# Attention and a routed expert layer on one core: fewer steps on which routing is advanced, a first token list over two groups, and first weights and transposes at other places of a DMA queue

## The chip, the core and the metric

The program runs on one core of a Trainium2 chip. Its engines work side by side, each on an instruction stream of its own, and wait for one another through semaphores: TensorE (PE in the profile, its weight loads PEld), VectorE (DVE), ScalarE (ACT), GpSimd (POOL) and SyncE (SP), which here issues nearly all DMA transfers. The metric is the device time of one execution in microseconds; lower is better.

## The reference

```python
def _attn_ref(q, k, v):                       # 8 x 8 heads, 1152 positions, 64 wide
    q_pool = q.reshape(B, H, S // 2, 2, D).mean(axis=3)       # 576 queries
    scores = scale * np.matmul(q_pool, k.transpose(0, 1, 3, 2))
    scores = scores - np.max(scores, axis=-1, keepdims=True)
    attn = np.exp(scores)
    attn = attn / (np.sum(attn, axis=-1, keepdims=True) + 1e-09)
    return np.matmul(attn, v)

def _moe_ref(x, modality_id, w_gate, modality_bias, w1, w2):  # x: 4608 tokens x 512
    logits = x @ w_gate + modality_bias[modality_id]
    e_idx = np.argmax(logits, axis=1)                         # one of 8 experts
    gate_w = softmax(logits)[arange(N), e_idx]
    for e in range(E):
        mask = e_idx == e
        h = np.maximum(x[mask] @ w1[e], 0.0)                  # w1: 512 x 1024
        out[mask] = gate_w[mask, None] * (h @ w2[e])          # w2: 1024 x 512
```

All is float32. The 64 heads' results, put side by side, are the 4608 tokens of 512 values that the second half routes, each to the one expert with the largest logit.

## The kernel before

**Attention.** Two heads share the 128 partitions, so there are 32 pairs (`npairs`), and each pair takes 18 steps (`NSTEP`) of a schedule written out by hand: 576 steps in all. PE computes the scores of a pair (`psc`, L906 and L907), takes the maximum of a coarser score pass for the pair after it (`pm`, L839 and L847, whose maxima DVE reduces at L840 and L848), and multiplies the exponentials with the values (`xp`, L965 to L967). Values in float32 are carried as pairs of 16-bit parts, a high and a low one. ACT makes the exponentials (`Pe`, L908) and part of their low parts (`Pl`, L889, and in pairs 26 and 27, `P_LIST`, some that DVE makes elsewhere); DVE makes the others (L891), the values' low parts (`vl`, L782, and `VS`, L798) and the output (L983 to L988). POOL adds the query halves (`split_q`, L658), splits them (`qh`, L667, `lo`, L695) and scales the values (`VH`, L786). SP copies all of these into the operands `B` and `QB` (`place`, L628), loads the next pairs (`load_kq`, `load_v`) and writes the row of maxima `mr` into `B` (`put`, L820). Since L907 reads that row, the pair's scores wait for it.

`hold` (L618) ties a POOL operation to a DVE one so that it comes after it; it is used for `split_q` and the first two `lo` of the pairs above `HELD` = 3.

**Scales.** Once per pair `scales` (L752) makes powers of two from a maximum, by four DVE operations `power_of` (L757): `sc` and its inverse `isc` for the values and the output, `isc` once more for the routing's table `scales`, and half of a tile `both` for the logits' weights.

**Logits.** After an odd pair, two heads' outputs are split (`split_x`, L935), turned by two DMA transposes (`turn_part`, L949) and multiplied with the routing weights (18 matmuls, L271) in the next pair. The first transpose is issued at once, at the end of the step of the ACT split; the second is left in `turns` and issued behind the next row DMA of `put`.

**Routing.** The tokens form four groups of 1152 (8 heads each, so a group is full after each 8 pairs). `Router` holds the code that turns logits into lists of tokens by expert: `setup` (L178, constants by 27 POOL operations, at once, at step 24), `route` of each group, and `first_list` (L569) after group 2: owners and sizes of the first six blocks of 256 tokens (`first_blocks`), the place of each token of three groups (`place`), and `listing`, per group three one-hot tables `ol` (L515), a table `o` (L521), two `r` (L526, L527) and nine matmuls (L547). These are generators in a list `side`. At the end of each of the 576 steps the first of them is advanced by a piece if its wait is over; what it yields is the wait in steps. A negative number is a step counted from the end: `T_LIST` = -127 puts the listing at step 449.

**The last pair and the experts.** At the step before the last pair, `gather_first` (L1579) runs what is left in `side` and issues the gather of the first block's tokens out of `xs`, a table in DRAM. At steps 1, 2, 3 and 3 of the last pair (`T_W0`) the four loads of the first expert's weights (512 KB each) are issued; ACT and DVE split them into parts at steps 6, 4, 10 and 11 (`split_first`, L1599 and L1601). Then 18 blocks of 256 tokens and half a block run through the two layers, PE by PE: `ph` (L1316 to L1318) and `po` (L1423 to L1425).

The order within each engine is the program's own: the schedule's steps decide it, and an engine takes no later instruction while an earlier one waits.

Of the kernel before, what the change touches and what calls it, by code (L numbers as in the profile page):

```python
# [9 lines left out]
F32 = mybir.dt.float32  # L10
# [12 lines left out]
P = 128  # L23
# [5 lines left out]
S = 1152  # L29
# [12 lines left out]
HELD = 3  # L42
BANK = W3 // 4
T_LIST = -127
# [77 lines left out]
T_W0 = (1, 3, 2, 3)  # L122
# [43 lines left out]
class Router:  # L166
# [11 lines left out]
    def setup(self, ids, w_gate, bias):  # L178
# [4 lines left out]
        for i in range(3):  # L183
            nc.gpsimd.tensor_copy(self.wg[:, :, i], wg)
            if i < 2:
# [5 lines left out]
        self.mid = con.tile([P, NTT], F32, name="mid")  # L191
        nc.gpsimd.tensor_copy(self.mid, idt[:, :, 0])
        self.up = con.tile([P, P], BF16, name="up")
        nc.gpsimd.memset(self.up, 1.0)
        nc.gpsimd.affine_select(out=self.up, in_=self.up, pattern=[[1, P]], compare_op=ALU.is_gt, fill=0.0, base=0, channel_multiplier=-1)
        self.id16 = con.tile([P, P], F16, name="id16")
        nc.gpsimd.tensor_copy(self.id16, self.ident)
        self.on = con.tile([P, P], BF16, name="on")
        nc.gpsimd.memset(self.on, 1.0)
        self.ie = self.iota("ie", E)  # L200
        self.ieE = self.iota("ieE", E, base=-E)
        self.lane16 = con.tile([P, P], BF16, name="lane16")
        nc.gpsimd.tensor_copy(self.lane16, self.iota("lane", P))
        self.part = self.iota("part", 1, cm=1)
        self.tile1 = self.iota("tile1", NTT, base=1)
        self.col = self.iota("col", 2 * (NBF - NA) + E)
        self.before = con.tile([P, E + 1, E], F32, name="before")
        nc.gpsimd.memset(self.before, 1.0)
        nc.gpsimd.affine_select(out=self.before, in_=self.before, pattern=[[1, E + 1], [-1, E]], compare_op=ALU.is_gt, fill=0.0, base=0,
                                channel_multiplier=0)  # L210
# [5 lines left out]
        self.added = {g: 0 for g in range(NTT // NT)}  # L216
        z = con.tile([P, NT, 2], F32, name="z")
        nc.gpsimd.memset(z, 0.0)
        nc.sync.dma_start(out=self.xs[T - NT * P:T, DM:XW].rearrange("(t p) d -> p t d", p=P), in_=z)
        self.pos = con.tile([P, NTT], F32, name="pos")  # L220
        self.exp = con.tile([P, NTT], F32, name="exp")
# [18 lines left out]
    def token_scale(self, p, isc):  # L240

        g, h = divmod(p, H)
        if h == 0:
            self.scales[g] = self.keep.tile([P, H], I32, name="scales")
        isc(self.scales[g][:, h:h + 1])
# [130 lines left out]
    def first_blocks(self):  # L376
# [29 lines left out]
        ef = sm.tile([P, NA], F32, name="ownA")  # L406
# [162 lines left out]
    def first_list(self):  # L569

        for _ in self.first_blocks():
            yield 1
# [1085 lines left out]
```

## Time and profile before

| | us |
|---|---|
| median of 3 runs (lowest, highest) | 1127.4 (1127.33, 1129.1) |
| the profiled execution | 1126.72 |
| its span, from first to last instruction | 1125.0 |
| PE busy, its mean granted clock | 1102.0, 0.997 |
| DVE, ACT, POOL busy | 972.0, 913.3, 414.2 |
| attention: a bare pair with logits, without | 22.16, 21.61 |
| the pair from 598.07 to 622.35, from 667.41 to 691.89 | 24.28, 24.48 |
| start of the last pair, of the experts' first matmul | 713.5, 735.3 |

How to read it: times are microseconds from the span's first instruction. A row of windows gives the stretch, its length, and for PE, PEld, DVE, ACT and POOL the busy time with the instruction count, then PE's granted clock, the share of the DMA engines and GB/s. A timeline row gives start, duration, engine, line, operation, what is written from what, and in brackets the idle time before it with what ended it. Pairs are cut here at the starts of ACT's squares (L743), one in each pair.

### The profile page before, as it was taken

What the parts mean: (1) busy time and instruction counts of PE and PEld (TensorE: products, weight loads), DVE (VectorE), ACT (ScalarE), POOL (GpSimd) and SP (SyncE); (2) the same over time, 40 slices, a digit from 0 to 9 for tenths busy, and PEclk for the clock granted to TensorE, in tenths of its full rate; (3) what the DMA queues carried; (4) which work ended last, traced back from release to release, by engine and by line L of the source; (5) the groups of instructions that cost most, each with busy time, mean ns of one, the idle gap of its engine ahead of it and who ended that gap; (6) DMA issues with size and microseconds to landing.
All of it is one profiled execution on the core that took longest, in us unless ns stands there. A gap on an engine that the chain in (4) does not pass through costs nothing.

```text
span 1125.0 us, 36836 instructions
## 1 busy us (share of the span) xinstructions
PE 1102.0 (98%) x15069; PEld 812.7 (72%) x15069; DVE 972.0 (86%) x1971; ACT 913.3 (81%) x1465; POOL 414.2 (37%) x408
## 2 busy tenths in 40 slices
PE   7999999999999999999999999999999999999997
PEld 3777777777777777777777777777667667667665
DVE  7999999999999999999999999877996766756755
ACT  5999999999999999999999998876556656655654
POOL 7753344355434444443445334115213112122111
PEclk9999999999999999999999999999999999999999
DMA  7777757768669578678687663499999999899993
GB/s 231 181 186 169 197 159 189 188 158 187 171 165 210 152 176 183 165 185 182 171 183 171 160 147 97 144 302 289 285 264 278 299 286 267 279 280 262 296 269 110
DMA packets 175522, 232.67 MB, mean 207 GB/s; under 512 B 92303, under 2 KB 126751, under 8 KB 175344
## 3 DMA queue, kind: packets, MB, share of 16 engines
q1 hardware_dynamic: 169254, 210.45, 71.4%
q0 software_dynamic: 6080, 19.78, 6.7%
q8 instruction: 120, 1.97, 0.8%
q14 instruction: 58, 0.48, 0.1%
q10 hardware_dynamic: 10, 0.00, 0.0%
HBM read 146.11 MB, written 18.99 MB: 147 GB/s over the span
## 4 chain that ended last, share of the span: by engine, by line
PE 80%; DVE 16%; DMA 2%; issue 1%; ACT 1%; SPq 0%; POOL 0%; POOLq 0%; DVEq 0%
PE psc L907 9%; PE psc L906 9%; PE pm L839 8%; DVE mp L840 8%; PE xp L965 6%; PE xp L967 6%; PE ph L1318 6%; PE ph L1316 6%; PE ph L1317 6%; PE xp L966 6%; PE po L1423 6%; PE po L1425 6%; PE po L1424 6%; DVE Pl L891 2%; DVE vl L782 1%; DVE mp L848 1%
## 5 line engine op out<-in xcount | busy, mean ns | idle before, releaser
L908 ACT ACTIVATE Pe<-psc 128x432 int32<-128x432 f32 x768 | 376.8, 526 | 40.6 <-PE psc L907 32.2
L840 DVE TENSOR_REDUCE mp<-pm 128x1 f32<-128x512 f32 x566 | 371.6, 684 | 16.8 <-PE pm L839 10.1
L965 PE MATMUL xp<-VH,Pe 128*128 128x65 f16 x2880 | 372.5, 193 | 0.0
L967 PE MATMUL xp<-VS,Pl 128*128 128x65 f16 x2880 | 371.9, 193 | 0.4 <-DVE Pl L891 0.4
L966 PE MATMUL xp<-vl,Pe 128*128 128x64 f16 x2880 | 370.6, 192 | 0.0
L966 PEld LDWEIGHTS <-Pe 128*128 128x128 f16 x2880 | 267.6, 98 | 87.6
L906 PE MATMUL psc<-B 128*128 128x432 f16 (+2 forms) x1152 | 304.1, 286 | 1.7 <-ACT Pe L908 1.5
L907 PE MATMUL psc<-B 65*128 65x432 f16 (+2 forms) x1152 | 304.7, 287 | 0.7 <-DMA B<-mr 0.5
L965 PEld LDWEIGHTS <-Pe 128*128 128x128 f16 x2880 | 272.0, 98 | 42.3 <-issue 4.7
L967 PEld LDWEIGHTS <-Pl 128*128 128x128 f16 x2880 | 266.5, 97 | 0.6 <-DVE Pl L891 0.6
L889 ACT ACTIVATE Pl<-Pe 128x1152 f16<-128x1152 uint16 (+1 forms) x190 | 219.2, 1154 | 6.0
L839 PE MATMUL pm<-hi,QB 128*128 128x512 f16 x566 | 213.8, 379 | 4.2 <-DVE mp L840 3.0
L1318 PE MATMUL ph<-xpart,w1l 128*128 128x256 f16 x544 | 148.3, 273 | 0.0
L1317 PE MATMUL ph<-xpart,w1h 128*128 128x256 f16 x544 | 148.3, 273 | 0.0
L1316 PE MATMUL ph<-xpart,w1h 128*128 128x256 f16 x544 | 148.3, 273 | 0.0
L786 POOL TENSOR_SCALAR VH<-rawv,sc 128x512 f16<-128x512 f32 (+1 forms) x60 | 103.6, 1736 | 76.2 <-PE pm L839 35.6
L907 PEld LDWEIGHTS <-B 65*128 65x128 f16 x1152 | 112.9, 98 | 25.2 <-issue 2.5
L906 PEld LDWEIGHTS <-B 128*128 128x128 f16 x1152 | 112.5, 98 | 7.9 <-issue 2.5
L1322 DVE SCALAR_TENSOR_TENSOR hl<-ph,hh 128x512 f16<-128x512 f32 x72 | 49.6, 689 | 76.6 <-ACT hh L1321 71.7
L1321 ACT ACTIVATE hh<-ph 128x512 f16<-128x512 f32 x72 | 43.0, 598 | 85.1 <-PE ph L1318 85.0
L1425 PE MATMUL po<-w2h,hl 128*128 128x512 f16 x288 | 109.2, 379 | 0.0
L1424 PE MATMUL po<-w2l,hh 128*128 128x512 f16 x288 | 109.2, 379 | 0.0
(288 smaller groups left out, 1881.3 us busy)
## 6 DMA issues: line engine op xcount, KB each, us to landing
w2r<-in_w_dram SPq DMA_DIRECT2D x76, 512.0 KB
w1r<-in_w_dram SPq DMA_DIRECT2D x72, 512.0 KB
rawv<-in_att_dram SPq DMA_DIRECT2D x32, 576.0 KB
B<-hi SPq DMA_DIRECT2D x128, 144.0 KB
rawq<-in_att_dram SPq DMA_DIRECT2D x31, 576.0 KB
rawk<-in_att_dram SPq DMA_DIRECT2D x31, 576.0 KB
B<-qh SPq DMA_DIRECT2D x128, 72.0 KB
B<-lo SPq DMA_DIRECT2D x64, 144.0 KB
```

The lines of the kernel that those rows point to most:

```text
L839: nc.tensor.matmul(pm, QB[p % 2][:, u], s["hi"][:, t * 512:(t + 1) * 512], start=True, stop=True)
L840: nc.vector.tensor_reduce(mp[:, u, t:t + 1], pm, op=ALU.max, axis=AX.X)
L889: nc.scalar.activation(low, rest, AF.Copy, scale=LOW)
L906: nc.tensor.matmul(o, b1[:, ks], b1[:, qs], start=True, stop=False, skip_group_check=True)
L907: nc.tensor.matmul(o, b2[:, ks], b2[:, qs], start=False, stop=True, skip_group_check=True)
L908: nc.scalar.activation(Pe[:, D + x0:D + x1], pt, AF.Exp, scale=1.0 / 16)
L965: nc.tensor.matmul(out, Ph[:, qs], vh[:, c, j, 0:D + 1], start=c == 0 and g == 0, stop=False, skip_group_check=True)
L966: nc.tensor.matmul(out[:, 0:D], Ph[:, qs], vl[:, c, j], start=False, stop=False, skip_group_check=True)
L967: nc.tensor.matmul(out, Pl[:, qs], vs[:, c, j, 0:D + 1], start=False, stop=c == NKC - 1, skip_group_check=True)
L1316: nc.tensor.matmul(o, hi[:, c, fs], xh[:, :, c], start=c == 0, stop=False)
L1317: nc.tensor.matmul(o, hi[:, c, fs], xl[:, :, c], start=False, stop=False)
L1318: nc.tensor.matmul(o, lo[:, c, fs], xh[:, :, c], start=False, stop=c == 3)
```

## The change

- `HELD` is 2 in place of 3: pair 3's q-addition and `lo` are held as well.
- `setup` becomes a generator in pieces with four steps between them (`ST`); its first piece runs at step 24 and the rest goes through `side`.
- The first list covers two groups (`GA`). `first_place` (sizes, owners and places) follows the routing of group 1, and `first_list`, now only the owners' last operation and the listing, that of group 2. `T_LIST` is gone.
- A piece of `side` comes only at eight steps of a pair (`QUIET`).
- `scales` makes two powers, the second straight into the routing's table, and POOL copies it to `both`.
- Both transposes wait in `turns` for the row DMA.
- The four weight loads are issued together, at the step 12 before the last pair, and behind the last pair's last key copy; their tiles are taken one step earlier.

```diff
-HELD = 3
+HELD = 2
+ST = 4
-T_LIST = -127
+GA = 2
+QUIET = (1, 2, 3, 4, 13, 14, 15, 16)
-T_W0 = (1, 3, 2, 3)
+T_W0 = -12
+T_R0 = -13
...
+        yield
+        self.up = con.tile([P, P], BF16, name="up")
+        nc.gpsimd.memset(self.up, 1.0)
+        nc.gpsimd.affine_select(out=self.up, in_=self.up, pattern=[[1, P]], ...)
+        yield ST
...
+    def first_place(self):
+
+        for _ in self.first_blocks():
+            yield PL
+        for _ in self.place(GA * NT, False):
+            yield PL
+
     def first_list(self):
 
-        for _ in self.first_blocks():
-            yield 1
-        for _ in self.place(3 * NT, False):
-            yield PL
-        yield T_LIST
+        self.ownA = self.con.tile([P, NA], I32, name="ownerA")
+        self.nc.vector.tensor_single_scalar(self.ownA, self.efA, float(E - 1), op=ALU.min)
+        yield 1
         acc = self.con.tile([P, 2, 2 * NA], F32, name="accA")
-        yield from self.listing(3, 2 * NA, acc)
+        yield from self.listing(GA, 2 * NA, acc)
...
-                move(s["B1"][half[i], kcol(j)], s["hi"][half[j]])
+                s["placed"] = move(s["B1"][half[i], kcol(j)], s["hi"][half[j]])
...
-        sc = sm.tile([P, 2], I32, name="sc")
+        sc, isc = sm.tile([P, 1], I32, name="sc"), on_scale(p)
-        power_of(sc[:, 0:1], half, -1, 205)
-        power_of(sc[:, 1:2], half, 1, 49)
-        on_scale(p, lambda o: power_of(o, half, 1, 49))
+        power_of(sc, half, -1, 205)
+        power_of(isc, half, 1, 49)
-        power_of(st[p - p % 2]["both"][r], half[r], 1, 49)
+        nc.gpsimd.tensor_copy(st[p - p % 2]["both"][r], isc[r])
...
-            turn_part(p, 0, xh)
+            turns.append(lambda: turn_part(p, 0, xh))
...
-                turns.pop(0)()
+                while turns:
+                    turns.pop(0)()
...
-    at(T_RT, 0, started)
+    def start_side():
+        setting = started()
+        next(setting)
+        side.insert(0, setting)
+
+    at(T_RT, 0, start_side)
...
+        def load_first(i):
+            with tc.issue_after(st[npairs - 1]["placed"].ins):
+                ahead[2](i, room[i + 1])
+
+        at(last + T_R0, 0, lambda: room.extend(pa.tile([P, S], F32, name="raw" + x) for x in "qqkkv"))
+        at(last + T_G0, 0, lambda: ahead[0](room.pop(0)))
...
-            at(last + T_W0[i], 0, lambda i=i: ahead[2](i, room[i]))
+            at(last + T_W0, 0, lambda i=i: load_first(i))
...
-                wait = t + (r or 1) if (r or 1) > 0 else NSTEP * npairs + r
+                wait = t + (r or 1)
+                while wait % NSTEP not in QUIET:
+                    wait += 1
...
-        ... in_=rt.xs[0:3 * NT * P if j < NA else T, :],
+        ... in_=rt.xs[0:GA * NT * P if j < NA else T, :],
...
                 side.append(rt.route(g, eng))
+                if g == GA - 1:
+                    side.append(rt.first_place())
```

The order of instructions, at three places. In all rows the name before the arrow is written, those behind it are read; the shape is what is written.

DVE, before, one stretch of the pair after group 2's last head, between the maxima `mp` of attention (the others from `L391` on are `first_blocks`: sums, remainders and owners):

```order
L391 TENSOR_REDUCE cumA<-wcumA 128x9
L840 TENSOR_REDUCE mp<-pm 128x1
L755 TENSOR_SCALAR half<-pm 128x1
L757 TENSOR_SCALAR sc<-half 128x1 x2
L757 TENSOR_SCALAR scales<-half 128x1
L757 TENSOR_SCALAR both<-half 64x1
L394 TENSOR_SCALAR left<-cumA 128x8
L848 TENSOR_REDUCE mp<-pm 128x4
L397 TENSOR_SCALAR left<-left 128x8
L398 TENSOR_SCALAR cutA<-cumA 128x9
L840 TENSOR_REDUCE mp<-pm 128x1 x2
L891 TENSOR_SCALAR Pl_120<-Pe_119 128x576
```

and the change, DVE, the stretch two pairs later, where the listing begins (`ol`, `o`: its tables; line numbers are those of the changed kernel):

```order
L358 TENSOR_REDUCE pos<-wide_15149 128x9
L588 TENSOR_SCALAR ownerA<-ownA 128x6
L853 TENSOR_REDUCE mp<-pm 128x1 x2
L904 TENSOR_SCALAR Pl_116<-Pe_115 128x576
L524 TENSOR_TENSOR ol_16631<-lof,lane_2085 128x384
L853 TENSOR_REDUCE mp<-pm 128x1 x2
L795 SCALAR_TENSOR_TENSOR vl<-rawv,sc,VH_127 128x512
L853 TENSOR_REDUCE mp<-pm 128x1 x2
L904 TENSOR_SCALAR Pl_118<-Pe_117 128x576
L853 TENSOR_REDUCE mp<-pm 128x1
L769 TENSOR_SCALAR half<-pm 128x1
L771 TENSOR_SCALAR sc<-half 128x1
```

The four powers are two, and the owners' arithmetic has left the late pairs (it stands after group 1's routing now); a listing of two groups is what remains there. Between two writes of the row `mr`, the number of DVE operations that belong to routing and lists was 2, 12, 17, 12, 8, 7, 12 in the last seven stretches, and is 5, 7, 4, 6, 7, 6, 7, 6, 5, 12 in the last ten.

POOL, one pair in the middle, before (`lo` of one pair, then the next pair's addition and values):

```order
L695 TENSOR_TENSOR lo<-rawk,hi 128x576
L298 TENSOR_TENSOR wide_5742<-wide_5742 128x72
L658 TENSOR_TENSOR rawq<-rawq 128x576
L786 TENSOR_SCALAR VH_127<-rawv,sc 128x8x64
L786 TENSOR_SCALAR VH_127<-rawv,sc 128x10x64
```

and the change:

```order
L778 COPY both<-scales 64x1
L310 TENSOR_TENSOR wide_5823<-wide_5823 128x72
L672 TENSOR_TENSOR rawq<-rawq 128x576
L799 TENSOR_SCALAR VH_127<-rawv,sc 128x8x64
L799 TENSOR_SCALAR VH_127<-rawv,sc 128x10x64
```

The copy stands ahead of the q-addition (L672) in POOL's queue, in every pair.

SP at the end, before (`B<-hi`: the last pair's key copies; `xs`: the store of two heads' outputs; `B_1_113<-mr`: the last pair's row; `raw...<-in_w`: the first weights):

```order
L628 DMA B_17353<-hi 64x1152 x4
L232 DMA xs<-x_16603 128x9x128
L949 DMA_TRANSPOSE xt_17619<-x_17056 128x9x128
L820 DMA B_1_113<-mr 1x9x128
L949 DMA_TRANSPOSE xt_17620<-x_17057 128x9x128
L1595 ISA
L1595 DMA rawq<-in_w_dram 128x1024
```

and the change:

```order
L642 DMA B_17312<-hi 64x1152 x4
L1616 TENSOR_LOAD ownerA
L1616 ISA x2
L1618 ISA
L1618 DMA rawq<-in_w_dram 128x1024
L1618 ISA
L1618 DMA rawk<-in_w_dram 128x1024
L244 DMA xs<-x_16564 128x9x128
L1618 ISA
L1618 DMA rawk<-in_w_dram 128x1024
```

Behind these come the fourth load, the row (L833) and the two transposes (L963): all four loads stand ahead of the row, and both transposes behind it.

More of the change, by code (lines that the diff above doesn't have):

```diff
@@ L190, in setup @@
         nc.sync.dma_start(out=idt.rearrange("p t w -> p (t w)"), in_=ids.bitcast(I32))
[L191 to L210, printed above, removed]
         self.base = self.keep.tile([P, E], F32, name="base")
@@ L216, in setup @@
         self.added = {g: 0 for g in range(NTT // NT)}
+        self.pos = con.tile([P, NTT], F32, name="pos")
+        self.exp = con.tile([P, NTT], F32, name="exp")
+        yield
+        self.up = con.tile([P, P], BF16, name="up")
+        nc.gpsimd.memset(self.up, 1.0)
+        nc.gpsimd.affine_select(out=self.up, in_=self.up, pattern=[[1, P]], compare_op=ALU.is_gt, fill=0.0, base=0, channel_multiplier=-1)
+        yield ST
+        self.id16 = con.tile([P, P], F16, name="id16")
+        nc.gpsimd.tensor_copy(self.id16, self.ident)
+        self.on = con.tile([P, P], BF16, name="on")
+        nc.gpsimd.memset(self.on, 1.0)
+        yield ST
+        self.ie = self.iota("ie", E)
+        self.mid = con.tile([P, NTT], F32, name="mid")
+        nc.gpsimd.tensor_copy(self.mid, idt[:, :, 0])
+        yield ST
+        self.ieE = self.iota("ieE", E, base=-E)
+        self.part = self.iota("part", 1, cm=1)
+        yield ST
+        self.lane16 = con.tile([P, P], BF16, name="lane16")
+        nc.gpsimd.tensor_copy(self.lane16, self.iota("lane", P))
+        yield ST
+        self.tile1 = self.iota("tile1", NTT, base=1)
+        self.col = self.iota("col", 2 * (NBF - NA) + E)
+        yield ST
+        self.before = con.tile([P, E + 1, E], F32, name="before")
+        nc.gpsimd.memset(self.before, 1.0)
+        nc.gpsimd.affine_select(out=self.before, in_=self.before, pattern=[[1, E + 1], [-1, E]], compare_op=ALU.is_gt, fill=0.0, base=0,
+                                channel_multiplier=0)
+        yield ST
         z = con.tile([P, NT, 2], F32, name="z")
@@ L219, in setup @@
         nc.sync.dma_start(out=self.xs[T - NT * P:T, DM:XW].rearrange("(t p) d -> p t d", p=P), in_=z)
[L220 to L221 removed]
+        yield ST
     def iota(self, name, n, base=0, cm=0):
@@ L244, in token_scale @@
             self.scales[g] = self.keep.tile([P, H], I32, name="scales")
-        isc(self.scales[g][:, h:h + 1])
+        return self.scales[g][:, h:h + 1]
     def turned(self, x, o):
@@ L405, in first_blocks @@
         yield
[L406 to L410 removed]
+        self.efA = self.con.tile([P, NA], F32, name="ownA")
+        nc.vector.tensor_reduce(self.efA, c3, op=ALU.add, axis=AX.X)
     def other_blocks(self):
@@ L461, in place @@
         yield
-        wide = lambda i: sm.tile([P, nt, E], F32, name=f"ohp{nt}_{i}") if late else sm.tile([P, 3, NT, E], F32, name=f"wide{i}").rearrange("p q t e -> p (q t) e")
+        wide = lambda i: sm.tile([P, nt, E], F32, name=f"ohp{nt}_{i}") if late else sm.tile([P, 3, NT, E], F32, name=f"wide{i}").rearrange("p q t e -> p (q t) e")[:, 0:nt]
         oh = wide(0)
@@ L627, in move @@
     def move(o, i):
-        nc.sync.dma_start(out=o, in_=i)
+        return nc.sync.dma_start(out=o, in_=i)
     half_q = lambda i: slice(i * 288, (i + 1) * 288)
```

15 lines of the change are left out of this document (3 added, 12 removed).

## The prediction

> **What bounds the kernel now.** I read the page first (busy times, then the chain that ended last), then a table of windows cut at the starts of ScalarE's square (L743, one per pair of heads), then the groups of instructions in the stretches that stand out, and the timeline at the places that the change touches. The page:
>
> ```profile
> PE 1102.0 (98%) x15069; PEld 812.7 (72%) x15069; DVE 972.0 (86%) x1971; ACT 913.3 (81%) x1465; POOL 414.2 (37%) x408
> ...
> PE 80%; DVE 16%; DMA 2%; issue 1%; ACT 1%; SPq 0%; POOL 0%; POOLq 0%; DVEq 0%
> ```
>
> PE is busy 98%, so any gain must come out of the 23 us in which it is not, or from work taken off it; but the chain runs through DVE for 16%, and that cannot be read from an average. The windows tell where (length, then busy time and instructions of PE, PE's loads, DVE, ACT, POOL; granted clock 1.00 throughout):
>
> ```profile
> 68.69:202.19 133.50, 132.12 (x2285) 102.10 (x2284) 128.71 (x276) 125.69 (x215) 55.77 (x42) 1.00 0.72 175
> 202.19:575.79 373.60, 373.38 (x6472) 289.21 (x6471) 358.72 (x802) 355.34 (x607) 165.77 (x139) 1.00 0.75 177
> 443.92:466.64 22.72, 22.68 (x404) 17.60 (x403) 22.14 (x54) 21.11 (x36) 9.80 (x9) 1.00 0.66 173
> 532.02:554.18 22.16, 22.16 (x394) 17.25 (x392) 21.14 (x48) 20.89 (x37) 9.30 (x7) 1.00 0.66 180
> 554.18:575.79 21.61, 21.61 (x372) 16.70 (x371) 20.66 (x46) 20.80 (x37) 9.29 (x7) 1.00 0.87 182
> 575.79:598.07 22.28, 22.28 (x394) 17.30 (x392) 21.41 (x51) 20.92 (x37) 11.34 (x12) 1.00 0.64 173
> 598.07:622.35 24.28, 22.92 (x391) 17.62 (x390) 22.68 (x61) 22.39 (x40) 12.44 (x13) 1.00 0.87 176
> 622.35:645.31 22.96, 22.80 (x395) 17.59 (x393) 22.24 (x60) 21.94 (x38) 9.55 (x7) 1.00 0.59 158
> 645.31:667.41 22.10, 21.08 (x363) 16.24 (x361) 21.66 (x53) 21.02 (x38) 7.89 (x6) 1.00 0.67 145
> 667.41:691.89 24.48, 23.22 (x395) 17.68 (x393) 24.19 (x56) 21.49 (x37) 9.88 (x7) 1.00 0.35 88
> 740.00:1110.00 370.00, 370.00 (x2617) 250.75 (x2616) 267.02 (x388) 227.86 (x293) 79.56 (x79) 1.00 0.98 277
> ```
>
> 532 to 576 are two bare pairs: 22.16 us with a group's 18 logit matmuls, 21.61 without, PE busy for all of it. These are PE's floors; DVE works 21.14 and 20.66 there, so it has about 1 us of room in a pair. The five pairs after 575.79 hold the last routing and the first list; they take 22.28 + 24.28 + 22.96 + 22.10 + 24.48 = 116.10 us against floors of 3 x 22.16 + 2 x 21.61 = 109.70: 6.40 us over. In 598 to 622 and 667 to 692 DVE's work (22.68, 24.19) is above the floor, by itself. The experts (740 to 1110) have PE busy without a gap and unchanged blocks, so whatever attention gains or loses arrives at the end one to one.
>
> The Trainium skill (Perfetto Trace Analysis, section Identifying the Most-Contended Engine) warns that a matmul's busy share is a poor measure of what limits. The trace agrees: the same 98% engine has pairs of 21.61 and of 24.48 us. By busy share alone the change would be worth little; that is a rival below.
>
> **The change part by part.** The sum is made against the profiled execution, 1126.72 us (span 1125.0 and 1.7 around it); the median of the runs shown is 0.7 above it, and I add that at the end.
>
> *The late pairs.* Groups of instructions of the five pairs together (count, then busy us and mean ns of one, then idle before and what ended it): what DVE does beside attention, and what PE waits for; the L839 row with x566 is that of the whole kernel:
>
> ```profile
> ...
> L515 DVE TENSOR_TENSOR ol<-lof,lane 128x384 bf16<-128x384 bf16 x5 | 3.4, 676 | 0.0
> ...
> L526 DVE TENSOR_TENSOR r<-o,tile 128x108 bf16<-128x108 f32 x2 | 0.9, 466 | 0.0
> ...
> L527 DVE TENSOR_SCALAR r<-o,part 128x108 bf16<-128x108 f32 x2 | 0.5, 268 | 0.0
> L521 DVE TENSOR_TENSOR o<-hif,col 128x108 f32<-128x108 f32 x2 | 0.5, 258 | 0.0
> ...
> L471 DVE SCALAR_TENSOR_TENSOR wide<-wide,cutA 128x216 f32<-128x216 f32 x1 | 0.4, 373 | 0.0
> ...
> L839 PE MATMUL pm<-hi,QB 128*128 128x512 f16 x90 | 34.1, 378 | 1.9 <-DVE mp L840 1.7
> ...
> L810 PE MATMUL pm<-ident,m 128*9 128x128 f32 x5 | 1.4, 277 | 1.0 <-DVE m L806 1.0
> ```
>
> ```profile
> L839 PE MATMUL pm<-hi,QB 128*128 128x512 f16 x566 | 213.8, 379 | 4.2 <-DVE mp L840 3.0
> ```
>
> 1.7 of the whole kernel's 3.0 us of waits of L839 on DVE's maxima fall in these five pairs. By the order of instructions the seven stretches between two row writes (L819) at the end of attention hold 2, 12, 17, 12, 8, 7, 12 side operations on DVE; afterwards the ten stretches there hold 5, 7, 4, 6, 7, 6, 7, 6, 5, 12. A small one costs 0.13 to 0.17 us of DVE's busy time: 15 more in 598 to 622 than in the bare pair made 2.0 (22.68 against 20.66), 6 more at 443.92 made 1.0. Twelve and 17 are far above 1 us of room. Placement now covers two groups, so its 0.37 us operations over 216 elements become 0.25, and one group's list (three `ol`, `o`, two `r`: 3 x 0.56 + 0.26 + 0.66 = about 2.6 us of DVE, less where `r` is 0.27, and nine matmuls) goes altogether. Stretches with six or seven small operations add 6 or 7 x 0.15 = 0.9 to 1.05 us: at the room, which the power operations below widen by 0.13. What will still be over: the routing's ten matmuls on PE (22.72 against 22.16: 0.55); the two stretches with list operands, `ol` 0.55 + `ol` 0.55 + `o` 0.26 + small ones = 1.7 each against 1.1 of room, 0.55 each, 1.1 together; ACT's extra lowerings in the pairs of 22.39 and 21.94, which stay, 0.3; local queueing 0.25. Together 2.2 of the 6.4: **-4.2 us**. The bounds: -5.0 if three quarters of the list operands' excess finds room in the pairs beside, and -2.5 if each of the pairs that now gets six or seven operations loses 0.35, most of what 645 to 667 lost with seven (0.49, 22.10 against 21.61): five times 0.35 on top of the 2.2.
>
> *Early.* Six pairs from 68.69 take 133.50 against 3 x (22.16 + 21.61) = 131.31: 2.2 over, though no routing is in them. Ahead of them stands the lump of 27 setup operations on POOL, and what it pushes (the timeline of POOL, then of DVE, with a `Pl` of the middle for comparison):
>
> ```profile
> 51.73 0.20 POOL L184 CAST wg<-wg 128x32 bf16<-128x32 f32 x1
> ...
> 59.25 0.40 POOL L218 MEMSET z<- 128x18 f32 x1
> ...
> 61.46 2.73 POOL L695 TENSOR_TENSOR lo<-rawk,hi 128x576 f16<-128x576 f32 x2
> ```
>
> ```profile
> 61.49 1.56 DVE L891 TENSOR_SCALAR Pl<-Pe 128x576 f16<-128x576 uint16 x1
> ...
> 316.95 0.45 DVE L891 TENSOR_SCALAR Pl<-Pe 128x576 f16<-128x576 uint16 x1
> ```
>
> From 51.73 to 59.65 POOL does little else, so `qh` and `lo` come late and `lo` starts together with DVE's lowering `Pl`, which takes 1.56 us in place of 0.45. The Trainium skill (SBUF — State Buffer, section Who interferes with whom) says of this that VectorE's two-port modes and GpSimd hold one shared port pair as an exclusive lock for a whole instruction; the row of 1.56 beside two `lo` of 2.73 together agrees. Afterwards the lump is 13, 7, 6 and 1 operations over four pairs, and one more pair's `lo` waits for a `Pl` on purpose (HELD). One collision of 1.1 us is saved, and 0.2 for what follows from it: **-1.3**, between 0.3 (the collision comes elsewhere) and 2.5 (all of the 2.2 and the collision's own pair).
>
> *The middle.* 17 pairs take 373.60 against 9 x 21.61 + 8 x 22.16 = 371.77: 1.8 over, of which two routings' matmuls are 1.1 and stay. Routing spread to the quiet steps and two power operations less per pair (0.13 us of DVE, which has room): **-0.4**, between +0.3 and -0.6.
>
> *The scale copy on POOL.* It stands ahead of the next q-addition in POOL's queue, so the addition now waits for `isc` (timeline of POOL, then of DVE):
>
> ```profile
> 313.70 1.41 POOL L658 TENSOR_TENSOR rawq<-rawq 128x576 f32<-128x576 f32 x1 [5.33 <-DVE Pl L891]
> 317.56 3.43 POOL L786 TENSOR_SCALAR VH<-rawv,sc 128x512 f16<-128x512 f32 x2 [2.44 <-PE pm L839]
> ```
>
> ```profile
> 314.60 0.21 DVE L757 TENSOR_SCALAR sc<-half 128x1 int32<-128x1 int32 x2
> 314.73 0.14 DVE L757 TENSOR_SCALAR scales<-half 128x1 int32<-128x1 int32 x1
> ```
>
> `isc` is there at 314.8 (now the second operation of the 314.60 row); a copy of 64x1 costs about the 0.20 of the `wg` cast above, so the addition runs from 315.1 to 316.5, before the `Pl` of 316.95 and well before VH. Cost nothing, covered by POOL's own gap of 2.44; if the cover goes it costs a second `Pl` collision, rival below.
>
> *The end.* SP's queue (start and duration of each issue), then a piece of the chain, a row of ACT, a group of DVE and one window:
>
> ```profile
> 695.72 2.47 SPq L628 DMA_DIRECT2D B<-hi  x4
> ...
> 708.78 0.79 SPq L820 DMA_DIRECT2D B<-mr  x1
> ...
> 711.17 0.39 SPq L1595 DMA_DIRECT2D rawq<-in_w_dram  x1
> ```
>
> ```profile
> 712.30 6.50 DMA rawk<-in_w_dram
> ```
>
> ```profile
> 718.83 1.06 ACT L1599 ACTIVATE w1h<-rawk 128x1024 f16<-128x1024 f32 x1 [0.91 <-DMA rawk<-in_w_dram]
> ```
>
> ```profile
> L1601 DVE SCALAR_TENSOR_TENSOR w1l<-rawk,w1h 128x1024 f16<-128x1024 f32 x2 | 2.4, 1224 | 0.9 <-ACT w1h L1599 0.9
> ```
>
> ```profile
> 712.00:714.00 2.00, 2.00 (x51) 1.73 (x49) 1.66 (x10) 1.99 (x4) 0.00 (x0) 1.00 1.03 299
> ```
>
> ACT's first weight split stands in its queue until `rawk` lands at 718.80 and holds the exponentials behind it. The four weight loads now follow the key copies that end at 698.2 (the first two ahead of the xs store, which waits for an eviction until 700), so the splits find their data. Of the 0.91 that ACT waits I count half as PE's loss, since PE has score blocks in hand when it begins: 0.5 gained, and 0.1 for a row no longer behind the first transpose: **-0.6**. Bounds: +1.0 if the row comes behind the weights a little, -1.5 if the 0.9 for which DVE's residues (1.22 each) wait on ACT comes free for PE too.
>
> Both transposes now stand behind the row on SP. They land perhaps 2 x 1.3 us later, and their reader is a pair's half away:
>
> ```profile
> 394.47 0.80 SPq L820 DMA_DIRECT2D B<-mr  x1
> 395.32 1.82 SPq L949 DMA_TRANSPOSE xt<-x  x1
> ```
>
> ```profile
> 410.32 0.60 PE L271 MATMUL pm<-wgs,xt 128*128 128x24 bf16 x18
> ```
>
> 13 us lie between: cost nothing. Behind them on SP stand the next pair's key copies; the last of those ended at 698.2 for a row at 708.78, so 2.6 us more leave them 8.
>
> The sum: -4.2 - 1.3 - 0.4 - 0.6 = -6.5; 1126.72 - 6.5 = 1120.2, and with the 0.7 to the median **1120.9 us**. The ends of the terms add up to -9.6 and -1.5; as they are not likely to fall together, the forecast's own range is 1118 to 1124.
>
> **The rivals.** (1) *The pieces are still too many for DVE.* Ten stretches are now nearly full where seven were, three of them bare before; if each of the eight with five to seven operations loses 0.35, they return 2.8: about 1123.5 (0.1 off for the power operations). For it: the 22.10 pair, 0.49 over with seven more than bare. Against it: the routing pair at 443.92 has six operations over the bare 48 and loses 0.04 beyond PE's own work (22.72 against 22.68).
> (2) *The last row queues behind the weights.* 2 MB of weights and 0.6 MB of the xs store are issued from 698.2 on one queue; at the 299 GB/s of 712 to 714 that is 2.6 / 0.30 = 8.7 us, until 706.9, against a row due at 708.78: 1.9 us to spare, less if the second pair of loads, behind the xs store, runs slower. A row that is 3.5 us late gives 1120.9 + 3.5 = about 1124.5 (the second half of the 2.6 MB at half the speed ends 4.4 us later, at 711.3, and the row's own transfer comes behind it). The Trainium skill (DMA: Bandwidth & Descriptors, section Queues, rings and completion order) says that each DMA engine takes descriptors in ring order, which would make this the outcome whenever the loads are not done; no row here shows a small transfer behind 2 MB.
> (3) *Slower: the copy pushes the q-addition onto `Pl` in every pair.* The place is POOL at 314.8 to 316.95. If the copy takes 0.45 us more than I think (waiting for `isc` through SBUF and back), the addition overlaps a `Pl`, which goes from 0.45 to 1.56. DVE then needs 20.66 or 21.14 - 0.13 + 1.1 = 21.6 or 22.1, right at the floors, and every side operation is paid in full: the 6.5 us are gone, and 17 pairs at about 0.2 add 3 to 4: about 1130.5. Against it: POOL's wait of 2.44 behind the addition.
> (4) *PE decides and little comes free.* The waits that the rows above name for PE in the five late pairs are only 1.7 + 1.0; if the rest of the 6.4 is PE's own order, the change brings the list's nine matmuls and little more: 1126 to 1127.4.
>
> **Chances.** Forecast 0.55; (1) 0.18; (2) 0.12; (3) 0.06; (4) 0.09. About 0.2%, 2.3 us, is what a measurement of this kernel can tell from no change. Below 1125.1 lie the forecast, (1) and more than half of (2): faster 0.80; (4) and the rest of (2) give same 0.13; (3) with a little else 0.07. The range reaches from the forecast's lower end, a little beyond 1118, to the upper part of (2) and the lower of (4): 1117.5 to 1126.0.
>
> **What would show it.** Right: the pairs after 576 take 22.2 to 22.9 with none at 24; no `Pl` of 1.5 us near 61; the first weights landed before ACT's split, which follows its neighbours without a wait; the row still issued by 708 of the old clock. Wrong: pairs from 480 to 576 above 22.4 (pieces too dense), PE waiting for `B<-mr` over 1 us in the last pair (weights ahead of the row), `Pl` with a mean well above 0.45 in steady pairs (the copy). The forecast as a whole falls if the five last pairs still exceed their floors by over 4 us.

## The result, and the profile after

| | before | changed |
|---|---|---|
| median of 6 runs each (lowest, highest) | 1127.07 us (1126.6, 1129.1) | 1120.82 us (1120.44, 1121.86) |
| ratio, with 95% interval | 1 | 0.9938 (0.9928 to 0.9948) |
| the profiled execution, its span | 1126.72, 1125.0 | 1120.44, 1118.7 |

The changed kernel is 0.6% faster. The forecast was 1120.9. That close a number hides that its four terms were not all right; where the time went is read first, and the agreement is taken apart further below. Tables and windows compare two single executions, of which the changed kernel's is the fastest of its six.

The page of the changed kernel:

```profile
PE 1100.3 (98%) x15060; PEld 812.3 (73%) x15060; DVE 962.1 (86%) x1900; ACT 910.9 (81%) x1465; POOL 413.0 (37%) x440
...
PE 87%; DVE 9%; ACT 1%; DMA 1%; issue 1%; POOL 0%; POOLq 0%; ACTq 0%; DVEq 0%
```

DVE's part of the chain has fallen from 16% to 9%. PE is as busy as it was; its 1.7 us less are not where most of the 6.3 us (1126.72 to 1120.44) came from. The windows, cut at the starts of the same squares (now L757), answer to the rows of the prediction:

```profile
199.90:573.20 373.30, 372.80 (x6472) 289.23 (x6471) 357.11 (x783) 355.30 (x607) 166.25 (x156) 1.00 0.73 177
...
331.96:353.58 21.62, 21.62 (x372) 16.72 (x371) 20.33 (x44) 20.81 (x37) 9.48 (x8) 1.00 0.78 177
...
573.20:595.36 22.16, 22.16 (x394) 17.25 (x392) 21.52 (x52) 20.91 (x36) 9.44 (x8) 1.00 0.67 181
595.36:618.39 23.03, 22.64 (x381) 17.32 (x380) 21.32 (x49) 22.15 (x40) 11.14 (x13) 1.00 0.80 170
618.39:641.07 22.68, 22.68 (x395) 17.61 (x393) 21.64 (x52) 21.89 (x39) 10.38 (x12) 1.00 0.66 174
641.07:662.24 21.17, 21.17 (x374) 16.49 (x372) 20.06 (x46) 20.59 (x37) 9.80 (x9) 1.00 0.66 151
662.24:684.89 22.65, 22.55 (x394) 17.40 (x392) 22.21 (x50) 21.13 (x36) 9.44 (x8) 1.00 0.40 99
```

The five late pairs take 111.69 us in place of 116.10, and none has 24. PE makes 1924 matmuls in them before and after; its idle time there falls from 3.8 us to 0.5, its busy time by 1.1. The middle is 373.30 in place of 373.60. From one profiled execution to the other, with the stretches summed:

| stretch | before | changed | difference | forecast |
|---|---|---|---|---|
| start to the first square | 19.99 | 18.89 | -1.10 | none |
| early, seven pairs from the third square (43.67) | 158.52 | 157.31 | -1.21 | -1.3 |
| the middle, 17 pairs | 373.60 | 373.30 | -0.30 | -0.4 |
| the five late pairs | 116.10 | 111.69 | -4.41 | -4.2 |
| last square to the first expert matmul | 43.25 | 43.16 | -0.09 | -0.6 |
| experts to the end | 389.86 | 390.61 | +0.75 | none |

Three terms came as forecast. The start (its edits begin behind it) and the blocks of the experts are as before, and what they moved nearly cancels; the gain at the end did not show.

The end, in the changed kernel, is this (SP's issues, then PE's waits between the last square and the experts):

```profile
695.61 1.29 SPq L1618 DMA_DIRECT2D rawv<-in_w_dram  x1
700.99 0.84 SPq L833 DMA_DIRECT2D B<-mr  x1
701.94 4.33 SPq L963 DMA_TRANSPOSE xt<-x  x2
```

```profile
PE psc L920 <- DMA B<-mr: 0.7, 1, 0.7
...
PE psc L919 <- ACT Pe L921: 0.4, 1, 0.4
PE xp L981 <- DVE Pl L904: 0.4, 1, 0.4
```

ScalarE no longer waits for its first weights. PE waits 0.7 for the last row instead, issued 4.1 us after the issue of the fourth load had ended, and the two transposes behind it now hold SP for 4.33.

The early pairs, POOL's timeline:

```profile
53.44 0.38 POOL L205 TENSOR_SCALAR_AFFINE_SELECT up<-up 128x128 bf16<-128x128 bf16 x1
53.78 0.65 POOL L681 CAST qh<-rawq 128x576 f16<-128x576 f32 x1
```

`qh` follows eight setup operations, at 53.78 and not at 59.30, and no `Pl` near it takes longer than 0.88 (it was 1.56).

### The profile page after: what moved, and what is told of

It reads as the page before. It is cut to its first block, busy times and chain, and to the rows that moved or that the text cites. A ratio compares the mean times of both kernels' runs of the same rounds, so it can differ in the third digit from the quotient of the medians.

```text
span 1118.7 us, 36764 instructions
## 1 busy us (share of the span) xinstructions
PE 1100.3 (98%) x15060; PEld 812.3 (73%) x15060; DVE 962.1 (86%) x1900; ACT 910.9 (81%) x1465; POOL 413.0 (37%) x440
## 4 chain that ended last, share of the span: by engine, by line
PE 87%; DVE 9%; ACT 1%; DMA 1%; issue 1%; POOL 0%; POOLq 0%; ACTq 0%; DVEq 0%
PE psc L920 11%; PE psc L919 11%; PE pm L852 9%; PE xp L979 7%; PE xp L981 7%; PE xp L980 6%; PE ph L1337 6%; PE ph L1339 6%; PE ph L1338 6%; PE po L1444 6%; PE po L1445 6%; PE po L1446 6%; DVE mp L853 5%; PE pm L860 1%; DVE Pl L904 1%; DMA B<-mr 1%
## 5 line engine op out<-in xcount | busy, mean ns | idle before, releaser
L709 POOL TENSOR_TENSOR lo<-rawk,hi 128x576 f16<-128x576 f32 (+1 forms) x68 | 82.9, 1222 | 78.7 <-ACT hi L693 58.4
L1444 PE MATMUL po<-w2h,hh 128*128 128x512 f16 x288 | 109.2, 379 | 0.0
```

## The experiments

Every kernel was timed beside runs of the kernel before on the same chip. The before's median moved between 1127.4 and 1128.2, so the ratios are compared, and the traces where the ratios' intervals overlap. The changed kernel was not timed again beside them: a comparison with it is one of two ratios. Waits and windows are of single executions. In the cuts of code, `...` stands for lines left out.

### Each part alone

The change falls into four parts that don't touch each other's lines. Each was put into the kernel before by itself.

**Routing alone** (`GA`, `QUIET`, places after group 1, the shorter list):

```diff
-T_LIST = -127
+GA = 2
+QUIET = (1, 2, 3, 4, 13, 14, 15, 16)
...
+                if g == GA - 1:
+                    side.append(rt.first_place())
...
```

> The kernel before with the routing part alone: pieces at eight steps of a pair, places after group 1, a first list over two groups; setup, scales, transposes and weights as before. Theory (the late term of the prediction): -4.2 us, 1122.9 against a before of 1127.1, nearly all of it in the five pairs after 576 us, and the pairs from 480 to 576 at most 0.6 longer together. Rival (PE's own order decides, little comes free): 1126 to 1127. Rival (pieces too many for DVE): 1124.5 to 1125.5, with 0.3 more in each of the eight pairs that now get pieces.

Measured: 1123.86, ratio 0.9969 (0.9958 to 0.9980), 3.5 us. The five late pairs took 112.46 (116.10 before): -3.64, nearly the forecast. Both rivals are out: most of the gain is there, and the pieces cost nothing net around the first routing (66.37 us for three pairs against 66.48). But two pairs of the middle are longer than 22.15 by 0.8 and 1.5, which no theory had, and PE's waits say why:

```profile
PE psc L910 <- DMA B<-mr: 2.3, 3, 1.3
```

The row of maxima came late, three times, up to 1.3 us; two of the three are in these pairs. This kernel still issues the first transpose ahead of the row.

**Setup in pieces and HELD alone:**

```diff
-HELD = 3
+HELD = 2
+ST = 4
...
-    at(T_RT, 0, started)
...
+    at(T_RT, 0, start_side)
```

> The kernel before with the setup in pieces and HELD 2 alone. Theory (the early term): -1.3 us, 1125.8, all of it before 110 us: the pair from 43.67 to 68.69 takes about 24.1 in place of 25.02, and the longest Pl falls from 1.56 to under 1.0. Rival: the 1.1 us by which the changed kernel's first square starts earlier (18.9 against 20.0) belongs to the change too, then 1124.7; if that is a landing that varies from run to run, the first square of this run can be at either place whatever the edit.

Measured: 1126.62, ratio 0.9992 (0.9983 to 1.0001), 0.9 us, with an interval that just includes no change; the trace is clearer. The pair from the third square takes 24.18 in place of 25.02, and the seven early pairs 157.62 in place of 158.52: -0.90. The long `Pl` at 61 is gone (one of 1.5 at the late collision stays, as before). The first square stands at 19.89, where the kernel before has it: the earlier start of the changed kernel is not this part's.

**First weights and transposes alone:**

```diff
-T_W0 = (1, 3, 2, 3)
+T_W0 = -12
...
-            turn_part(p, 0, xh)
+            turns.append(lambda: turn_part(p, 0, xh))
...
```

> The kernel before with the first weights behind the last key copies and both transposes behind the row, alone. Theory of the prediction: -0.6 us, 1126.5, the split on ScalarE no longer waiting 0.91 for its weights. Rival from the changed kernel's trace: the wait for the row, or for DVE ahead of the last lowerings, takes the place of the wait removed, and the time is the same within 0.2. Rival (2) of the prediction: the row lands later than 5.4 us after its issue, and the time is 1 to 3 us longer.

Measured: 1126.07, ratio 0.9987 (0.9978 to 0.9995), 1.5 us, more than twice the forecast, with an interval that reaches down to it. From the last square to the experts it is 42.60 in place of 43.25: -0.65, the forecast's 0.6, and PE waits for no row at all in this kernel. But the same stretch is 42.51, 43.03 and 43.50 in the three other parts alone, whose edits leave weights, row and transposes where they were. ScalarE's wait for `rawk` is 0.91 before and 0.40, 0.55 and 1.23 in these three, and the stretch follows it: what taking the wait away is worth differs from one execution to the next. The row of this kernel was issued 5.2 us after the last load's issue, since the late pairs were still slow: rival (2) does not hold there. Between the first and the last square it takes 0.45 less. Late rows don't explain that: PE waits for none there in the profile of the kernel before either.

**Two powers and POOL's copy alone:**

```diff
...
-        power_of(st[p - p % 2]["both"][r], half[r], 1, 49)
+        nc.gpsimd.tensor_copy(st[p - p % 2]["both"][r], isc[r])
```

> The kernel before with two powers in place of four, the copy on POOL, alone. Theory: DVE's busy time in a bare pair falls by 0.3 (20.66 to 20.33, as in the changed kernel), and since PE bounds those pairs, 0 to -0.4 us: 1126.7 to 1127.1. Rival (the q-addition pushed onto Pl): Pl's mean well above 0.45 in steady pairs and 3 to 4 us longer, 1130 to 1131.

Measured: 1129.11, ratio 1.0010 (1.0001 to 1.0019): slightly slower, outside both expectations. Bare pairs still take 21.62. DVE's busy time is 20.34 in the two at 202 and 556 us, as expected, and 20.70 in the one at 334. There two `Pl` take 0.73 and 0.85 in place of 0.45: the first runs beside the end of the q-addition, the second beside `qh`. Rival (3) thus happens in single pairs, and not in every one. The row waits (1.6 us, 3 of them, one ahead of the middle) account for most of what this execution lost in the middle, and the pair at 647 lost 0.6, which the last one gained back. The part's worth is settled below by taking it out.

The four ratios multiply to 0.9958; all parts together give 0.9938. The difference is some 2 us, about what the errors of the five ratios allow together; the next runs show that the parts don't simply add.

### One part undone

**The first transpose ahead of the row again**, in the changed kernel:

```diff
-            turns.append(lambda: turn_part(p, 0, xh))
+            turn_part(p, 0, xh)
```

> The changed kernel with the first transpose issued at once again, ahead of the row on SP; everything else as changed. Theory (formed from the single parts): the row waits on its way behind that transpose in some pairs, so PE's waits for B<-mr come back, 1 to 2.5 us in three or so of the 14 pairs with logits in the middle: 1.0 to 1.6 us slower than the changed kernel, about 1122.2, with a wider spread. Rival (the prediction: moving the transposes costs and gains nothing): the same as the changed kernel within 0.3 us, no waits for the row in the middle.

Measured: 1127.05, ratio 0.9995 (0.9985 to 1.0005). Nearly all of the change's gain is gone: by the ratios one line costs some 6.4 us. The direction is the theory's, the size four times it; the trace shows how much of it is late rows. The waits of this kernel, then three of its pairs with logits (22.16 where no row is late):

```profile
PE psc L920 <- DMA B<-mr: 4.6, 6, 2.0
```

```profile
398.15:421.13 22.98, 22.32 (x394) 17.36 (x393) 21.25 (x47) 21.23 (x37) 10.52 (x12) 1.00 0.66 176
442.74:465.35 22.61, 22.32 (x394) 17.35 (x393) 21.69 (x49) 21.20 (x37) 9.69 (x9) 1.00 0.67 181
531.46:554.40 22.94, 22.32 (x394) 17.35 (x393) 21.55 (x52) 21.22 (x37) 9.43 (x8) 1.00 0.67 182
```

From the first to the last square it loses 2.4 us against the changed kernel, of which PE's waits for four rows are 2.3. From there to the experts it loses 2.7. With the weights, the transpose and the row in this order the last row comes 2.0 late (0.7 in the changed kernel), which makes 1.3 of it. The other 1.4 are a slower clock, from where that wait ends:

```profile
711.10:714.50 3.40, 3.34 (x38) 2.77 (x38) 0.61 (x1) 1.59 (x3) 1.25 (x2) 0.50 0.61 165
```

For 3.4 us the granted clock is 0.50. In the kernel with pieces at all steps (below) PE waits longer, 2.9 us, and the clock stays at 1.00, so that the wait alone brings the slow clock is not shown. The start (0.9 later) and the tail (0.5) make up the rest of its span's 6.5; the line has no part in them that a trace shows.

**The weights behind the row again**, in the changed kernel (`T_W0` and the tiles as before):

```diff
-T_W0 = -12
+T_W0 = (1, 3, 2, 3)
...
```

> The changed kernel with the four first weights loaded behind the last row again, at steps 1, 3, 2, 3 of the last pair. Theory of the prediction: +0.5 us, and ScalarE's first split waits about 0.9 for rawk. Theory formed from the traces: the wait of ScalarE comes back, but PE's wait of 0.7 for the last row goes, or the delay is used up before the last lowerings: within 0.2 us of the changed kernel.

Measured: 1123.48, ratio 0.9964 (0.9950 to 0.9977). By the ratio 2.6 per mille slower than the changed kernel (intervals just apart), by the traces equal where the edit works: 43.13 from the last square to the experts against 43.16. ScalarE waits 1.1 for `rawk` again and PE 0.8 for the `Pe` behind it, and the row's wait of 0.7 goes. Of its 1.6 us more span, 1.5 stand ahead of the first square, where the program is the same. So the second theory holds in the place where it can be read, and the ratio's remainder is left open.

**Four powers again**, in the changed kernel:

```diff
...
-        nc.gpsimd.tensor_copy(st[p - p % 2]["both"][r], isc[r])
+        power_of(st[p - p % 2]["both"][r], half[r], 1, 49)
```

> The changed kernel with four powers on DVE again and no copy on POOL. Theory of the prediction: 0 to +0.6 us against the changed kernel, since DVE has room in bare pairs and lacks it in the late ones (0.13 to 0.3 us in each of four). Rival, from the single part that made the kernel 1.1 to 1.7 us slower alone: POOL's copy costs by itself, and this kernel is 1 to 1.5 us faster than the changed one, about 1119.5.

Measured: 1121.32, ratio 0.9946 (0.9933 to 0.9960). Its median is within the theory, and the rival is out: between the first and the last square it takes 666.11 against 666.00. DVE's busy time in the same bare pair is 20.66 against 20.33, so the part gives DVE 0.3 us per pair that bare pairs cannot use. But the even total hides two differences. The five late pairs take 112.27 against 111.69, so there the part is worth 0.6, as the theory had it. The middle takes 372.66 against 373.31, so there the part costs 0.65, nearly all of it in two pairs behind a group's routing. One of them, in the changed kernel and then with four powers:

```profile
463.30:485.54 22.24, 22.00 (x382) 17.00 (x381) 21.08 (x50) 21.00 (x37) 10.21 (x11) 1.00 0.78 169
```

```profile
464.20:486.10 21.90, 21.90 (x382) 17.00 (x381) 21.34 (x52) 20.97 (x38) 10.25 (x11) 1.00 0.75 170
```

The matmuls are the same in number. With two powers DVE has less to do and PE is still held up, by 0.24 in this pair; through which wait was not followed to its start.

**Pieces at all steps**, in the changed kernel:

```diff
-QUIET = (1, 2, 3, 4, 13, 14, 15, 16)
+QUIET = tuple(range(18))
```

> The changed kernel with pieces of routing allowed at all 18 steps; places still after group 1, list still over two groups. Theory (the gain comes from work taken out of the late pairs and spread over many): the early places come as a lump between 485 and 530 us, 12 to 17 operations in a stretch again, 1.5 to 3 us slower than the changed kernel, about 1123. Rival (the eight steps themselves do nothing, the shorter list does it all): within 0.5 us of the changed kernel.

Measured: 1128.01, ratio 1.0004 (0.9991 to 1.0016). Without the eight steps all the rest together is worth nothing. The lump of places is about where the theory put it, begins a pair earlier, and is dearer:

```profile
465.22:487.97 22.75, 21.61 (x371) 16.68 (x370) 22.22 (x52) 21.36 (x38) 9.55 (x8) 1.00 0.68 157
487.97:511.53 23.56, 23.16 (x395) 17.54 (x392) 23.28 (x57) 21.37 (x36) 9.46 (x8) 1.00 0.68 179
...
599.67:623.86 24.19, 22.94 (x391) 17.65 (x390) 22.72 (x57) 22.43 (x41) 11.26 (x13) 1.00 0.73 167
```

The places are a lump in the pairs after 465 (DVE 23.28 in one pair), and the last routing is one in the pair at 600, which takes 24.19 (24.28 before the change). Against the kernel before, the five late pairs still gain 2.4 us (113.73 for 116.10), and the middle loses 2.6 (376.23 for 373.60): the shorter list has moved the work forward, and only the eight steps keep it from being a lump there. Between first and last square the kernel loses 5.1 us against the changed one. Whether eight other steps would do as well was not run. Here the last row comes later still:

```profile
702.21 1.18 SPq L1618 DMA_DIRECT2D rawv<-in_w_dram  x1
707.10 0.86 SPq L833 DMA_DIRECT2D B<-mr  x1
708.06 6.20 SPq L963 DMA_TRANSPOSE xt<-x  x2
```

```profile
PE psc L920 <- DMA B<-mr: 3.1, 2, 2.9
```

With 3.7 us between the last load's issue and the row, PE waits 2.9; with 4.1 (the changed kernel) 0.7; with 5.2 (four powers again) 0.4, and none with 5.2 in the part alone. The distance is not all: in the kernel with ten copies (below) it is 3.7 too, and PE waits 0.8. Rival (2) is a real mechanism, and the changed kernel stands at its edge.

### The row and the weights, and what the copy may cost

**Two loads behind the row:**

```diff
-            with tc.issue_after(st[npairs - 1]["placed"].ins):
+            with tc.issue_after(st[npairs - 1]["placed" if i < 2 else "put"].ins):
...
```

(`put` is the row's DMA; the loads split at steps 4 and 6 stay ahead of it.)

> The changed kernel with two of the four weight loads (those split at steps 4 and 6) ahead of the last row as changed, and the other two behind the row and the transposes. Theory (the row lands late behind 2 MB of weights): PE's wait of 0.7 for B<-mr in the last pair goes, the two transposes are issued in under 3 us in place of 4.3, and the splits still find their data: 0.5 to 0.8 us faster than the changed kernel, 1120.2. Rival (the row waits for something else): the wait stays, no difference.

Measured: 1120.09, ratio 0.9932 (0.9918 to 0.9945); not to be told from the changed kernel by the ratio. The trace answers the question:

```profile
696.30 0.35 SPq L1619 DMA_DIRECT2D rawk<-in_w_dram  x1
...
703.82 0.84 SPq L833 DMA_DIRECT2D B<-mr  x1
704.76 2.81 SPq L964 DMA_TRANSPOSE xt<-x  x2
```

The wait for the row is gone, the transposes are issued in 2.81, and from the last square to the experts it takes 42.26 against 43.16: -0.9. Of this 0.7 are PE's waits (1.5 in the changed kernel, 0.9 here). That is the 0.6 of the forecast, and a little more: the gain at the end had gone to the row behind the weights. The Trainium skill (DMA: Bandwidth & Descriptors, section Queues, rings and completion order) says that each DMA engine consumes descriptors in ring order. These rows agree, in that the row is no longer late once two of the loads stand behind it.

**ScalarE's extra lowerings where the list now is:**

```diff
-P_LIST = {26: 0, 27: 0}
+P_LIST = {29: 0}
```

> The changed kernel with ScalarE's extra lowerings moved from pairs 26 and 27 to pair 29, where the list's tables are now made. Theory (ScalarE sets the two pairs of 23.03 and 22.68, DVE the one of 22.65): 595 to 618 falls by 0.5 to 0.9 to about 22.2, the next by 0.4, the pair at 662 by 0.3: 1.2 to 1.6 us faster than the changed kernel, 1119.4. Rival (PE's route matmuls and DVE set those pairs): within 0.4 us of it, or slower by what DVE then lacks, up to 0.5.

Measured: 1119.24, ratio 0.9925 (0.9912 to 0.9939), the fastest median here, though its interval overlaps the changed kernel's. Its late pairs:

```profile
596.90:618.53 21.63, 21.63 (x372) 16.71 (x371) 20.86 (x48) 20.82 (x38) 11.20 (x13) 1.00 0.77 165
618.53:640.82 22.29, 22.29 (x393) 17.36 (x392) 21.90 (x55) 21.05 (x37) 10.55 (x12) 1.00 0.72 192
640.82:662.71 21.89, 21.89 (x382) 17.05 (x381) 21.11 (x49) 20.92 (x37) 9.79 (x9) 1.00 0.67 147
662.71:686.01 23.30, 23.20 (x403) 17.90 (x401) 22.62 (x50) 22.17 (x38) 9.40 (x8) 1.00 0.41 99
```

The first of them takes 21.63 (23.03 in the changed kernel), but that is less a gain than it looks. PE's work has moved between the cuts: 372 matmuls in place of 381 here, and 382 and 403 in place of 374 and 394 in the last two, which are longer by 0.7 each. In the four pairs together it is 89.11 against 89.53, so the move gains about 0.4 there, net of what pair 29 pays with ScalarE at 22.17. From 595 or 597 to the experts it is 130.98 against 132.69, 1.7 us faster; the other 1.3 stand behind the last square, 0.7 of them PE's wait for the row, which now has 5.2 us from the last load and is not late. So the edit helps, but for the larger part not in the way of the theory. No extra lowerings at all would be the next try; that was not run.

**Both edits:**

> Both edits together. Theory: the sum of the two, 1.7 to 2.2 us faster than the changed kernel, about 1118.8. Rival (the earlier last pair meets the row's landing again, as in the kernel with all steps, where the row was 3.7 us behind the last load): the gain of the lowerings is given back at the row, 1119.8 to 1120.3.

Measured: 1119.93, ratio 0.9933 (0.9920 to 0.9947). From the same square to the experts 131.00: the same as the lowerings alone. The gains don't add, and not for the rival's reason: with the lowerings moved, the last row was not late any more, so there was nothing for the second edit to give.

**The copy ten times:**

```diff
-        nc.gpsimd.tensor_copy(st[p - p % 2]["both"][r], isc[r])
+        for _ in range(10):
+            nc.gpsimd.tensor_copy(st[p - p % 2]["both"][r], isc[r])
```

> The changed kernel with the copy to both made ten times in every pair in place of once, 1.3 us more on POOL ahead of the q-addition. It prices rival (3). Theory: the q-addition, which ended 0.25 us ahead of a Pl, now overlaps it, that Pl takes about 1.5 us in place of 0.45 in each of some 29 pairs, DVE's busy time in a bare pair goes from 20.33 to 21.4, and the time is 3 to 7 us longer, 1124 to 1128. Rival (DVE's room and the depth of the queues hide it): under 1 us longer.

Measured: 1152.86, ratio 1.0221 (1.0207 to 1.0235): 25 us over the kernel before, 32 over the changed one, far above what was expected. Its timeline, of POOL and then of DVE in one pair of the middle:

```profile
375.90 2.56 POOL L779 COPY both<-scales 64x1 int32<-64x1 int32 x10 [6.56 <-DVE scales L771]
378.42 1.41 POOL L672 TENSOR_TENSOR rawq<-rawq 128x576 f32<-128x576 f32 x1
379.81 3.56 POOL L800 TENSOR_SCALAR VH<-rawv,sc 128x512 f16<-128x512 f32 x2
```

```profile
377.97 0.45 DVE L905 TENSOR_SCALAR Pl<-Pe 128x576 f16<-128x576 uint16 x1
...
382.33 0.46 DVE L905 TENSOR_SCALAR Pl<-Pe 128x576 f16<-128x576 uint16 x1
383.40 0.90 DVE L812 TENSOR_SCALAR VS<-VH 128x1152 f16<-128x1152 f16 x1 [0.60 <-POOL VH L800]
```

The ten copies take 2.56, a step of 0.26 each, where 0.14 was assumed. The addition comes 2.3 us later and misses the `Pl` of 377.97 altogether, so the expected collision isn't there. What hurts is behind it in POOL's queue: VH ends at 383.37, DVE stands idle 0.60 for it in the middle of its own queue, and `VS` then takes 0.90 in place of 0.45 beside the next POOL operation. This is no single case: DVE waits for VH 22 times, 17.2 us in all, and 22 of its 31 `VS` take over 0.6 (2 of 31 in the changed kernel). A bare pair takes 22.67 in place of 21.62, one with logits 23.01 in place of 22.16: 0.85 to 1.05 us in most pairs.

In the changed kernel POOL is close to that, in one pair:

```profile
312.65 0.18 POOL L778 COPY both<-scales 64x1 int32<-64x1 int32 x1 [6.82 <-DVE scales L771]
312.79 0.32 POOL L356 TENSOR_TENSOR wide<-wide,oh 128x72 f32<-128x72 f32 x1
313.07 1.40 POOL L672 TENSOR_TENSOR rawq<-rawq 128x576 f32<-128x576 f32 x1
```

The copy costs 0.18 and the addition ends at 314.47, 0.25 before a `Pl`, VH 0.9 before `VS`. In two other pairs (`Pl` at 248.44 and 424.3) the addition does reach a `Pl`, which takes 0.73, and these pairs still take 21.63 and 21.62. One copy is free of that kind of cost; by the 0.26 of a step, some four more would not be (an estimate, not run).

## Why the prediction was right, and where not

- **The late pairs, -4.2:** right. 4.41 in the changed kernel, 3.64 with routing alone. One floor was mis-sized: the pair at 645 to 667 can take 21.17, not 21.61, so the excess of before was 6.8 and what remains is 2.4, close to the 2.2 of the forecast. What was not seen is what the early places cost if they come at any step. The prediction gave the shorter list 2.6 us of DVE and the spreading the rest; with all steps allowed the late pairs still gain 2.4, and a lump in the middle takes 2.6 back. The gain is kept by the eight steps.
- **Early, -1.3:** right in size (1.21, and 0.90 alone) and in mechanism: `qh` 5.5 us earlier, the `Pl` of 1.56 gone. The remaining excess of those pairs (22.57, 22.37, 22.27) stayed.
- **The middle, -0.4:** right by the two profiles (0.30), but not by the powers, which cost 0.65 there and are worth 0.6 in the late pairs instead. The kernel before happened to lose nothing to late rows in the middle of its profiled execution (its one late row, 0.5, stands ahead of the first square); the three single parts with the same order of transposes lost 0.8 to 2.3 behind that square. So 0.30 is in part luck too.
- **Both transposes behind the row, nothing:** this is the step that failed. The prediction looked only at whether the transposes would come too late for their reader, and they don't. What the first of them did to the row behind it was counted for the last pair alone, with 0.1. Put back, it costs the changed kernel its gain by the ratios (0.9995 against 0.9938). In the traces late rows are 2.3 us of this between the first and the last square and 1.3 at the end; another 1.4 there are the slower clock, whose cause stays open.
- **The end, -0.6:** mechanism right, and the part alone shows 0.65, though the stretch moves as much between kernels without the edit. In the changed kernel it was used up by rival (2), which the prediction had at 0.12: the last row, earlier by what the late pairs gained, met the weights. Two loads behind it bring 0.9 back. The prediction's 1.9 us to spare came from a transfer rate and a row at its old distance from the loads; that distance shrank to 4.1 us.
- **Rival (1), 0.18:** out. The four pairs ahead of the late ones, from 485 to 573 us, take 87.66, where the same four took 87.55 before.
- **Rival (3), 0.06:** it did not come but in single pairs, rightly for the gap on POOL, and its place and price were wrong. The larger danger is VH ahead of `VS`, not the addition on `Pl`, and with VH 2.3 us later the price is up to 1.05 us per pair, not 0.2.
- **Rival (4), 0.09:** out. In the late pairs PE's idle time fell from 3.8 us to 0.5 with the same matmuls; its share of 98% over the whole was no limit.
- **The agreement to 0.1 us is luck in part.** The start gave 1.1 that was not forecast, experts and tail took 0.75, and the end kept 0.5 back. What carries the forecast is the sum of the late and the early terms, 5.6 of the 6.3 us.

## What to carry to other kernels

When work is moved off a full engine, count how much each stretch between two of its deadlines then holds: spreading the same operations over more stretches brought some 5 us between the first and the last square here; moving some of them forward without spreading won 2.4 in one place and lost 2.6 in another. And a small transfer that an engine waits for should be looked at as a member of its queue: ask what large transfers stand ahead of it, and what will when everything before it becomes faster. A term that cancels in the sum is not confirmed by the sum (the two powers are worth 0.6 in one stretch and cost as much in another); only the parts by themselves, and each taken back, told which lines carried the time.

## What was not expected of the hardware

A row of 2.2 KB lands late behind a transpose or behind weights, so that PE waits 0 to 2.9 us, and differently from one pair to the next of the same program: in the changed kernel with the transpose put back, PE waited for five rows behind the first square, and not for the others. In the kernels with the row ahead of the transposes, PE waited for none between 20 us and the last pair.

The first square starts anywhere between 18.68 and 20.43 us in the fourteen profiled executions, whatever the edit. In the two main ones a key load of the first pair lands at different times, though it is issued at the same time:

```profile
6.11 0.51 ACT L679 CAST hi<-rawk 128x384 f16<-128x384 f32 x1 [0.99 <-DMA rawk<-in_att_dram]
```

```profile
5.37 0.51 ACT L693 CAST hi<-rawk 128x384 f16<-128x384 f32 x1 [0.17 <-DMA rawk<-in_att_dram]
```

The first row is of the kernel before, the second of the changed one. Why it lands so differently was not tried; a comparison of two single profiles can be wrong by that much.
